# Moving one unit's leftover token rows into a seven-product pass of the last unit, and placing attention visits by phase

## Chip, core and metric

The kernel runs on one core of one Trainium2 chip. The metric is the device time of one execution in microseconds (us). Before the change it is 1392.92 us, the median of three runs from 1391.83 to 1393.26 us.

## What is computed

Attention with normalized queries and keys, followed by a feed-forward network with a squared ReLU. All inputs of the attention are float32; the two weight matrices arrive as 64-bit floats, and the kernel turns them into float32 on the chip.

```python
# q, k, v: 8 batches x 12 heads x 448 rows x 64; g_q, g_k: 64
q_n, k_n = rmsnorm(q, g_q), rmsnorm(k, g_k)
attn = softmax(q_n @ k_n.T / 8)            # per batch and head
x = (attn @ v) as rows of 3584 tokens x 768
h = maximum(x @ w_in, 0)                   # w_in: 768 x 2048
out = (h * h) @ w_out                      # w_out: 2048 x 768
```

## The kernel before, in words

**Units.** Two batches of 448 tokens make a unit, u = 0 to 3. The attention of unit 0 runs alone at the start. After that the feed-forward network of unit u runs on TensorE between the "visits" of the attention of unit u + 1, one or two visits for each pair of heads. The network of unit 3 has no attention left to run beside and comes alone at the end.

**Blocks and phases.** The generator `ffn` (line 943) goes through four blocks of the 2048 hidden columns. A block has a first phase, in which `x @ w_in` makes two by two tiles `hid`, and a second phase, in which `hid @ w_out` is added to accumulators `acc` in SBUF. Both phases use a scheme of seven products in place of eight (Strassen's, in Winograd's form): `PRODUCTS` names them P1 to P7, the banks of PSUM ("roles") that they share, and the sums of the left and right sides that they read. Sums of left sides (S1, S2, S4, and S3 written over a21) are made on GpSimd by `hidden_sum` (line 1141, instructions of line 1151). Those of the weights are made by `make_sum` (line 1508, instructions of line 1514), on VectorE and GpSimd in turn. A float32 matmul shows as two passes in the trace, so a product of the second phase (two matmuls of 384 columns, line 1251) is four passes.

**Rests.** 448 rows are three tiles of 128 and 64 more. The second phase works on pairs of tiles, one of each batch (NT = 3 pairs). The 64 rows left over of each batch are put together as one tile, the unit's rest. Units 1 and 2 store their rests in DRAM block by block (`keep_rests`, line 1173). Unit 3 loads them (`bring_rests`, line 1181), forms their sums on GpSimd (`add_rests`, line 1203) and multiplies the two as one more pair of tiles, tt = NT, after its own three pairs. Units 0 and 3 multiply their own rest without the scheme in `multiply_rest` (line 1165): four parts times two halves, eight matmuls, sixteen passes a block. In unit 0 these open the second phase. In unit 3 they stand in two groups of four matmuls among the products of the first tile pair (`FIRST_OF_BLOCK`).

**The order of the work.** Every engine runs its instructions in the order in which the program emits them. The order is planned with costs: a product of the first phase costs 18, one of the second 10. `run` (line 1586) takes steps of the generator until a sum of costs is reached, and after every step it also lets through one piece of the deep weight forms (lines 1474 and 1492), one sum of weights, delayed work such as loads, and tasks of the attention. `place` (line 1572) says at which cost each visit of the attention stands. For unit 0 the 24 visits stand at equal distances of the whole cost:

```python
if u == 0:
    return COST * x / unit
```

A block of unit 0 costs 502 before the change: 252 for the first phase and 250 for the second, of which 40 are the rest.

**Conversions.** The weights of blocks 1 to 3 are converted to float32 beside unit 0. `convert` (line 1520) splits a piece on ScalarE (lines 1405, 1406, 1408), joins the piece before it on VectorE (lines 1419, 1438), and asks for the load of the piece after next (`load_weights`, lines 1386 and 1391), which is issued two steps later, or at the latest when it is needed. A block has 16 conversions; the list `late` (line 1553) sets the cost at which each is made, 31.4 apart, eight in a second phase and eight in the first phase after it.

Of the kernel before, what the change touches and what calls it, by code (L numbers as in the profile page):

```python
# [14 lines left out]
F32 = mybir.dt.float32  # L15
# [8 lines left out]
P = 128  # L24
# [201 lines left out]
def program(ctx, tc, rows, v, g, wide, ones, moe_w_in, moe_w_out, out, shift):  # L226
# [690 lines left out]
    FIRST_OF_BLOCK = ["P1", "rest0", "P5", "P4", "P6", "P2", "rest1", "P3", "P7"]  # L917
# [8 lines left out]
    COST_SECOND = (NT * 7 + 4) * COST_OUT  # L926
    COST = NF // 2 * 7 * COST_IN + NBLK * COST_SECOND
    COST_SHORT = NT * 7 * COST_OUT
    LATER = NBLK * (7 * 11 * COST_DEEP + COST_SHORT)
    KEPT = range(1, B // 2 - 1)  # L930
    assert len(KEPT) == 2
# [11 lines left out]
    def ffn(u):  # L943

        accs = []
        for blk in range(NBLK):
# [8 lines left out]
            if u == B // 2 - 1:  # L955
                bring_rests(blk)
                add_rests()
# [195 lines left out]
    PARTS = [(0, 0), (1, 0), (0, 1), (1, 1)]  # L1153
    PARTS_BY_ROW = [(0, 0), (0, 1), (1, 0), (1, 1)]

    def out_of(u, blk):
        return [u * NF // 2 + 2 * blk + t for t in range(2)]

    def multiply_rest(u, blk, hid, places, some, acc=None, halves=range(2)):

        w_sb = [out_sb[n] for n in out_of(u, blk)]
        for half in halves:
            ps = places[half][:, 0:HALF]
            for a, t in some:
                nc.tensor.matmul(  # L1165
                    ps, lhsT=hid[a].rearrange("p t e s -> p t (e s)")[:, t, ds(NT * P, P)],
                    rhs=w_sb[t][:, 2 * a + half, :],
                    start=(a, t) == PARTS[0], stop=(a, t) == PARTS[-1],
                )
            if acc is not None:  # L1170
                add_to(acc[:, ts(half, HALF)], ps, blk == 0)
# [9 lines left out]
    def bring_rests(blk):  # L1181

        if not extra:
            for name in ("11", "12", "S3", "22", "S1", "S2", "S4"):
                some = att.tile([P, S], F32, name="wT", tag="wT", bufs=8)
                extra[name] = some[:, 0 : 2 * P].rearrange("p (t n) -> p t n", t=2)
            extra["accs"] = [
                room.rearrange("p x g h d -> p (x g h d)")[:, 0:DM] for room in rows.rooms
            ]
        for u, names in zip(KEPT, (("11", "12"), ("S3", "22"))):  # L1190
            for a, name in enumerate(names):
                nc.sync.dma_start(extra[name], kept[u][blk, :, a])

    def add_rests():
# [10 lines left out]
    def second_products(u, blk, hid, sums_, accs):  # L1205

        split, final = u in KEPT, u == B // 2 - 1
        if blk == 0:
            accs.extend(new_acc() for _ in range(2 * NT if split else 2 * NT + 1))
# [688 lines left out]
```

## Time and profile before

| what | value |
|---|---|
| median of three runs | 1392.92 us |
| the profiled execution: its own time | 1394.38 us |
| the profiled execution: span from first to last instruction | 1392.6 us |
| mean granted TensorE clock in the span | 0.998 |
| TensorE idle, 10 to 150 us (attention of unit 0 alone) | 1.9 us |
| TensorE idle, 150 to 490 us (network of unit 0) | 3.8 us |
| TensorE idle, 490 to 1105 us (units 1 and 2) | 8.3 us |
| TensorE idle, 1105 us to the end (unit 3 and the last stores) | 7.9 us |
| rests of unit 0, line 1165, four blocks | begin at 177.6, 264.7, 356.0, 443.4 us |

How to read it: the span is that of one profiled execution, and 1.8 us lie outside it in that execution's own time. A stage's idle time is its length less the time in which TensorE is busy. In the rows of the trace, "x16" is the number of instructions that were merged; the figure ahead of the engine is the time from the first one's start to the last one's end; a time in brackets is idle time just before, with what ended it. A bank is a bank of PSUM.

### The profile page before, as it was taken

The numbers are of one execution on the slowest core, as the hardware profiler recorded it, in microseconds if no ns is written. First come the engines' busy times: TensorE is split into PE (matmuls) and PEld (weight loads), VectorE is DVE, ScalarE is ACT, GpSimd is POOL, SyncE is SP. The second block draws the span as 40 slices with busy tenths as digits, with TensorE's granted clock in tenths as the row PEclk, the third lists the DMA queues.
The fourth block names the chain that finished last, engine by engine and source line by source line (L and its number), as shares of the span: only waits on it lengthen the run. The fifth ranks groups of instructions, "written<-read, shape, count | busy, mean of one in ns | idle before, by whom it ended". The sixth has DMA issues, their size and how long they took to land.

```text
span 1392.6 us, 19474 instructions
## 1 busy us (share of the span) xinstructions
PE 1363.3 (98%) x6320; PEld 845.7 (61%) x6320; DVE 807.2 (58%) x1635; ACT 608.3 (44%) x1118; POOL 789.6 (57%) x794
## 2 busy tenths in 40 slices
PE   7999999999999999999999999999999999999997
PEld 3333444444444466676758586676768677868684
DVE  4786545867758755555556755455546642445444
ACT  6885477757666244353434244442434032202020
POOL 5668664746656868576667877566745630303030
PEclk9999999999999999999999999999999999999999
DMA  5566746968769875664739475755527442424223
GB/s 147 149 168 169 203 117 159 264 179 219 233 155 284 231 215 162 187 173 141 204 86 279 140 225 149 211 153 176 146 86 239 142 165 103 135 90 149 78 90 100
DMA packets 385588, 233.36 MB, mean 168 GB/s; under 512 B 272452, under 2 KB 354244, under 8 KB 381380
## 3 DMA queue, kind: packets, MB, share of 16 engines
q1 hardware_dynamic: 385184, 231.95, 57.7%
q8 instruction: 52, 0.85, 0.3%
q14 instruction: 60, 0.49, 0.1%
q10 hardware_dynamic: 292, 0.07, 0.0%
HBM read 174.59 MB, written 57.34 MB: 167 GB/s over the span
## 4 chain that ended last, share of the span: by engine, by line
PE 81%; POOL 4%; DVE 4%; DMA 3%; issue 3%; SPq 2%; ACT 2%; POOLq 0%; ACTq 0%; DVEq 0%
PE bank L1251 30%; PE bank L1042 20%; PE bank L986 8%; PE bank L446 5%; PE bank L536 5%; PE bank L550 4%; PE bank L435 4%; PE bank L1165 2%; POOL sum L473 2%; PE bank L585 1%; DMA qk<-in_k_dram 1%; PE bank L611 1%; SPq L326 1%; SPq L318 1%; PE bank L571 1%
## 5 line engine op out<-in xcount | busy, mean ns | idle before, releaser
L1042 PE MATMUL bank<-xT,in_sb 128*128 128x224 f32 x1344 | 289.3, 354 | 2.9 <-ACT part L1031 2.3
L1251 PE MATMUL bank<-out_sb,hid 128*128 128x384 f32 x768 | 272.5, 488 | 2.2 <-POOL out_sb L1514 1.4
L1345 DVE TENSOR_TENSOR acc<-acc,bank 128x384 f32<-128x384 f32 x312 | 166.6, 548 | 164.6 <-PE bank L1251 138.1
L1042 PEld LDWEIGHTS bank<-xT,in_sb 128*128 128x128 f32 x1344 | 252.6, 190 | 15.0 <-ACT wT L454 5.6
L454 ACT ACTIVATE wT<-bank,rr 128x448 f32<-128x448 f32 x288 | 163.5, 631 | 155.1 <-PE bank L435 92.7
L1251 PE MATMUL bank<-out_sb,sums 128*128 128x384 f32 x576 | 207.2, 490 | 1.3 <-DVE acc L1345 0.9
L1251 PEld LDWEIGHTS bank<-out_sb,hid 128*128 128x128 f32 x768 | 144.7, 190 | 104.5 <-issue 5.6
L204 POOL TENSOR_TENSOR rr<-ms,minus_half 128x8 f32<-128x8 f32 (+1 forms) x96 | 146.0, 1521 | 73.7 <-DVE ms L197 63.8
L1251 PEld LDWEIGHTS bank<-out_sb,sums 128*128 128x128 f32 x576 | 107.7, 190 | 86.3 <-issue 4.3
L1027 DVE TENSOR_TENSOR hid<-hid,bank 128x224 f32<-128x224 f32 x312 | 111.0, 383 | 83.9 <-PE bank L1042 79.1
L986 PE MATMUL bank<-xT,in_sb 128*128 128x448 f32 x336 | 131.9, 546 | 0.1
L473 POOL TENSOR_TENSOR sum<-sum,wT 128x448 f32<-128x448 f32 (+1 forms) x96 | 110.6, 1173 | 8.1 <-ACT wT L454 6.6
L986 PEld LDWEIGHTS bank<-xT,in_sb 128*128 128x128 f32 x336 | 62.1, 190 | 69.0 <-issue 60.2
L446 PE MATMUL bank<-qT,kT 64*128 64x448 f32 (+1 forms) x492 | 100.5, 571 | 1.9 <-DVE qT L409 1.1
L473 POOL TENSOR_TENSOR sum<-wT 128x448 f32<-128x448 f32 x48 | 55.8, 1183 | 69.8 <-ACT wT L454 69.8
L1099 ACT ACTIVATE hid<-hid 128x448 f32<-128x448 f32 x96 | 55.0, 573 | 66.7 <-DVE hid L1027 48.5
L435 PE MATMUL bank<-qT,kT 64*64 64x448 f32 x552 | 77.0, 547 | 1.9 <-ACT wT L454 1.9
L1042 PE MATMUL bank<-more,in_sb 128*128 128x224 f32 x288 | 76.2, 357 | 1.4 <-DVE hid L1037 1.4
L550 PE MATMUL bank<-wT,vt 64*64 64x448 f32 x576 | 74.3, 548 | 0.0
L1039 ACT COPY hid<-bank 128x448 f32<-128x448 f32 x24 | 12.8, 532 | 137.3 <-PE bank L1042 137.3
L369 ACT ACTIVATE qT<-qT,g 128x448 f32<-128x448 f32 x34 | 22.6, 665 | 113.7 <-DVE qT L367 113.7
L446 PEld LDWEIGHTS bank<-qT,kT 64*128 64x128 f32 (+1 forms) x492 | 34.9, 166 | 60.4 <-issue 36.8
(140 smaller groups left out, 2059.1 us busy)
## 6 DMA issues: line engine op xcount, KB each, us to landing
out_sb<-out_forms SPq DMA_DIRECT2D x24, 1536.0 KB, 9.9
in_sb<-in_deep SPq DMA_DIRECT2D x64, 384.0 KB, 4.2
in_sb<-in_deep SPq DMA_DIRECT2D x80, 256.0 KB, 4.1
words<-in_moe_w_in_dram SPq DMA_DIRECT2D x32, 384.0 KB, 3.8
words<-in_moe_w_out_dram SPq DMA_DIRECT2D x32, 384.0 KB, 3.6
out_forms<-out_sb SPq DMA_DIRECT2D x8, 1536.0 KB, 7.5
qk<-in_q_dram SPq DMA_DIRECT2D x96, 96.0 KB, 2.6
qk<-in_k_dram SPq DMA_DIRECT2D x96, 96.0 KB, 2.7
```

What stands on the lines that cost most here:

```text
L204: self.nc.gpsimd.tensor_tensor(out=self.rr[i][:, x, 0 : self.count(i)], in0=ms, in1=self.minus_half.to_broadcast(list(ms.shape)), op=ALU.pow,)
L435: nc.tensor.matmul(sc[ds(half * D, D)], lhsT=turned[i, 1][ds(e * D, D), ds(m * P + half * D, D)], rhs=turned[i, 0][ds(e * D, D), :], start ...
L446: nc.tensor.matmul(sc[some], lhsT=turned[p, 1][r, keys], rhs=turned[p, 0][r, :], start=True, stop=True,)
L454: nc.scalar.activation(new_weights((i, m), e), sc, AF.Exp, scale=rows.rr[i][:, 1, 2 * m + e : 2 * m + e + 1],)
L473: nc.gpsimd.tensor_tensor(out=sums[i, e][some], in0=left[some], in1=weights[key_of(i, m), e][some], op=ALU.add)
L536: nc.tensor.matmul(values_bank(i)[ds(e * D, D), :], lhsT=lasts[i % 2][mine, e, :] if m == NJ else values[i][:, m, e, :], rhs=weights[key_o ...
L550: nc.tensor.matmul(bank[ds(e * D, D), :], lhsT=values[i][keys, n, e, :], rhs=weights[(i, n), e][keys], start=n == 0, stop=n == NJ - 1 and ...
L986: nc.tensor.matmul(ps, lhsT=w_sb[:, IN.index(left), c, :], rhs=forms[u, c][right], start=first and c == 0, stop=c == NK - 1, skip_group_ch ...
L1027: nc.vector.tensor_tensor(out=quarter(name, n), in0=quarter(base, n), in1=ps, op=ALU.add)
L1042: nc.tensor.matmul(ps, lhsT=left, rhs=right, start=start, stop=stop, skip_group_check=True)
L1251: nc.tensor.matmul(ps, lhsT=extra[left][:, t] if tt == NT else lefts[left][:, t, ts(tt, P)], rhs=w_sb[t][:, OUT.index(right), :], start=fi ...
L1345: nc.vector.tensor_tensor(out=acc, in0=acc, in1=ps, op=ALU.add)
```

## The change

- Unit 0 no longer multiplies its rest. It stores it in DRAM as units 1 and 2 do, two transfers a block (`KEPT` now takes in unit 0). The delayed entry for it is made at the beginning of the second phase.
- Unit 3 multiplies two pairs of rests, those of units 1 and 2 (tt = NT) and those of units 0 and 3 (tt = NT + 1), both by the seven products. `multiply_rest` is gone. Its tile pairs come in the order NT, 0, 1, NT + 1, 2. The pair NT is multiplied in `FIRST_ORDER`, and after its P1 come the left sums of the block and then the sums of the second pair, four more instructions on GpSimd.
- Unit 3 brings six tiles a block in place of four. The room for the second pair's five tiles comes from buffers `wT`, `qT` and `kT` of the attention.
- The accumulators of the rests of units 0 and 3 move from `acc` to a second part of the rooms of `rows`. Their rows are stored as two transfers of 64 rows for each accumulator, at the end of unit 3 in place of the ends of units 0 and 3.
- In unit 3 all copies out of PSUM in block 0 are ScalarE's; before, those of the first tile pair were VectorE's.
- In unit 0 visits are placed by phase, three at equal distances in each first phase (84 apart) and three in each second phase (70 apart, which is after every seventh product). Conversions are 27.1 apart in second phases and 22.5 apart in first phases, where the eighth now falls 162 into the phase of 252.

```diff
-    COST_SECOND = (NT * 7 + 4) * COST_OUT
-    COST = NF // 2 * 7 * COST_IN + NBLK * COST_SECOND
-    COST_SHORT = NT * 7 * COST_OUT
+    COST_FIRST, COST_SHORT = 2 * 7 * COST_IN, NT * 7 * COST_OUT
+    COST = NBLK * (COST_FIRST + COST_SHORT)
...
-    KEPT = range(1, B // 2 - 1)
+    KEPT, REST_PAIRS = range(B // 2 - 1), ((1, 2), (0, 3))
...
-                bring_rests(blk)
-                add_rests()
+                bring_rests(blk, hid)
+                add_rests(0)
...
             make_sums(0, 1, 2, 3)
-            for some in (PARTS[:3], PARTS[3:]):
-                multiply_rest(u, blk, hid, roles, some, accs[-1] if (1, 1) in some else None)
-                yield len(some) * COST_OUT
-            turn_roles(2, 1, 0)
+            later.append([5, lambda: keep_rests(u, blk, hid)])
...
-                    ps, lhsT=extra[left][:, t] if tt == NT else lefts[left][:, t, ts(tt, P)],
+                    ps, lhsT=lefts[left][:, t, ts(tt, P)] if tt < NT else extra[tt - NT][left][:, t],
...
-        for tt in range(0 if split else NT + final):
-            order = SECOND_ORDER if tt or not u else FIRST_OF_BLOCK
-            for name in order:
...
+        for tt in () if split else (NT, 0, 1, NT + 1, 2) if final else range(NT):
+            for name in FIRST_ORDER if final and tt == NT else SECOND_ORDER:
+                product(tt, name, roles[PRODUCTS[name][0]][:, 0:HALF], nc.scalar)
+                if final and (tt, name) == (NT, "P1"):
+                    yield from sums_behind_first()
+                    add_rests(1)
                     continue
...
-    every = block / ahead
+    every = ((COST_SHORT - 2 * COST_OUT) / (ahead // 2 - 1), (COST_FIRST - 4 * COST_IN) / (ahead // 2))
     late = deque(
-        block + 2 + every * (n - 2 * tile_pieces) for n in range(len(all_pieces) - ahead)
+        n // ahead * block + (COST_FIRST, block)[m] + 2 + every[m] * (n % (ahead // 2))
+        for n in range(len(all_pieces) - ahead) for m in [n % ahead * 2 // ahead]
     )
...
         if u == 0:
-            return COST * x / unit
-        block = LATER // NBLK
...
+            offsets = [COST_FIRST * n // 3 for n in (1, 2, 3)]
+            offsets += [COST_FIRST + COST_SHORT * n // 3 for n in (1, 2, 3)]
+            block = COST // NBLK
```

## The prediction

> **What bounds the kernel now.** I read the page's busy times first.
>
> ```profile
> PE 1363.3 (98%) x6320; PEld 845.7 (61%) x6320; DVE 807.2 (58%) x1635; ACT 608.3 (44%) x1118; POOL 789.6 (57%) x794
> ```
>
> TensorE (PE) is busy 98% of the span, no other engine above 58%. [...] So I looked in the timeline at what follows what.
>
> ```profile
> 1164.11 9.20 PE L1251 MATMUL bank<-out_sb,wT 128*128 128x384 f32 x28
> 1173.13 0.54 PE L1042 MATMUL bank<-xT,in_sb 128*128 128x224 f32 x2
> ```
>
> The pair of rests in unit 3: 28 passes between 1164.11 and 1173.13 us, no idle time in brackets. One pass of 384 columns takes 9.02 / 28 = 0.322 us of TensorE's queue, although a row gives 0.49 us as its mean (neighbours overlap). Weight loads (0.19 us each) lie under it. The row decides: a pass removed from such a stretch is worth 0.322 us, not nothing and not 0.49.
>
> Then the busy times by stretch: first phase of unit 0's block 3, its second phase, block 0 of unit 3.
>
> ```profile
> 399.50:443.40 43.90, 43.90 (x142) 18.90 (x140) 30.63 (x52) 34.24 (x62) 23.48 (x19) 1.00 0.78 217
> 443.40:486.30 42.90, 41.62 (x142) 20.80 (x140) 31.28 (x60) 9.39 (x17) 36.10 (x36) 1.00 0.85 253
> 1102.50:1172.90 70.40, 70.40 (x283) 53.20 (x282) 28.95 (x61) 19.20 (x39) 22.41 (x24) 1.00 0.36 125
> ```
>
> After the stretch and its length the columns are PE, PEld, DVE, ACT and POOL. TensorE fills all three but for 1.28 us in the second. The nearest rivals are ACT in first phases (34.2 of 43.9; 36.1 of 44.1 in block 1, 37.2 of 47.5 in block 2) and POOL in block 3's second phase (36.1 of 42.9).
>
> **The change part by part.**
>
> *Passes.* Unit 0 loses 16 a block, 64 in all. They stand on the path:
>
> ```profile
> 443.42 5.43 PE L1165 MATMUL bank<-out_sb,hid 128*128 128x384 f32 x16
> 448.69 2.74 PE L1251 MATMUL bank<-out_sb,hid 128*128 128x384 f32 x8
> 451.27 2.74 PE L1251 MATMUL bank<-out_sb,sums 128*128 128x384 f32 x8
> 454.36 0.91 PE L1251 MATMUL bank<-out_sb,hid 128*128 128x384 f32 x2 [0.34 <-DVE acc L1345]
> 455.95 0.91 PE L1251 MATMUL bank<-out_sb,hid 128*128 128x384 f32 x2 [0.69 <-POOL out_sb L1514]
> ```
>
> 64 x 0.322 = 20.6 us off. Unit 3 loses its own 16 a block and gains seven products of four passes, 28: 12 x 4 = 48 more, 48 x 0.322 = 15.5 us. Net 16 passes, **-5.2 us**. No other matmul changes, and the instruction orders of units 1 and 2 on TensorE are the same in both programs.
>
> *What the rest covered.* In the rows above, 5.2 us of passes lie between the first phase and the first product that needs a sum. Without them P5 starts 2.58 us after the first phase and its visit end (P1 and P2, 1.29 us each), P6 at 3.87, P4 at 5.16.
>
> Left sums: in block 3, where P1 would start at 443.42, POOL makes S1 from 443.99 to 445.40 and S2 to 446.48; P5 is due at 446.00 and P6 at 447.29. Slack 0.6 and 0.8 us. Block 1 has the same 0.6; blocks 0 and 2 have more. [...] After the change two VectorE derivations of deep forms come back to back at just this place. By the row S1 takes 1.00 us undisturbed and 1.41 in blocks 1 and 3, beside such work, and the slack above has 1.41 in it already. [...] I take 0 by the row, and up to 0.5 us in each of blocks 1 to 3 for the range.
>
> Weight sums: both waits of 0.69 to 0.70 us on POOL's out_sb (blocks 1 and 3) are T4, made after the rest had begun. In the new order the last conversion stands 162 into the first phase and T4 is emitted at its last product, ahead of the left sums on POOL. **-1.4 us**, certain within a few tenths.
>
> Evacuation: with three banks P6 waits for P1's addition to leave its bank, 2.58 us later. VectorE's order at the boundary loses a weight sum and a join (0.55 each) and gains a derivation (0.55); it was done with the visit's work 2.7 us after the boundary (446.1). P1's addition lands at about +2.5 against +3.87. Nothing is added there.
>
> *VectorE's queue in block 3.* SP sends nine piece loads at this boundary, then the blocks for the keys' transpose, which stands in VectorE's queue ahead of additions that free banks:
>
> ```profile
> 446.89 4.59 SPq L892 DMA_DIRECT2D in_sb<-in_deep  x9
> 451.66 1.96 SPq L326 DMA_DIRECT2D qk<-in_k_dram  x2
> ```
> ```profile
> 458.42 0.65 DVE L367 STREAM_TRANSPOSE kT<-qk 128x448 f32<-128x448 f32 x1 [4.12 <-DMA qk<-in_k_dram]
> ```
>
> The blocks land 15.0 us after the boundary. VectorE's 4.12 us of waiting now lie under a visit. In the new order the transpose comes after P4's addition, at +7.1, with P3's and P7's additions behind it; the next tile pair's P2 needs P3's bank at +13.7 (seven products 9.0, visit 3.4, P1 1.3). If the blocks still land at +15.0, P2 waits for the transpose and the addition until 16.3: 2.6 us, and some tenths at P5. But the large store of weight forms that went out just ahead (440.32) now goes out three products earlier, and SP should be through its loads 2 to 3 us sooner: +12.5, no wait. Bounds 0 and 3.5; I take 1.5, less the 0.34 shown above: **+1.2 us**. In blocks 1 and 2 no piece loads lie there, and the blocks are asked for 4 us after the boundary: nothing.
>
> *Conversions closer together.* In first phases of blocks 1 to 3 the steps with a conversion go from 1, 2, 4, 6, 8, 9, 11, 13 to 1, 2, 3, 4, 6, 7, 8, 9. Each load is issued two steps after the conversion two earlier, so four of eight are now issued in the step that needs them. Landing takes 3.6 to 3.8 us (page, part 6), so ACT may wait for them. Cover: the copy behind has 4.7 us (two products) before its bank is needed, later copies 6 to 8 because a visit lies between. Walking ACT's new order with the old durations, it catches up at the visit 15 us in and lags about 3 us by the last conversion, at 30 of 44 us; then it has 14 us without conversions. I take **+0.5 us**, bounds 0 and the rival below. In second phases conversions go from 31.4 to 27.1 apart; ACT has 28.3 us of work at most there, in 37.8: nothing.
>
> *POOL in block 3*: 36.1 us of work in 42.9 - 5.2 = 37.7. It stays under TensorE, but what it makes for unit 1's start comes up to 3 us later against TensorE; there a 1.9 us stall on ACT's weights exists already. I take +0.3, bounds -1 and 2.
>
> *Transfers.* Eight stores of rests (128 KB, 2.0 us) and eight more loads (2.1 us) pass through SP's queue, 16 x 0.6 us. In unit 0 the store is ahead of the q loads of the next pair by 1.2 us; a pair has two visits, 27 us. In unit 3 a block's loads have the whole first phase: nothing. The loads for the next block wait for the pair NT + 1, which ends 9 us before the block does, earlier than now.
>
> *Unit 3 otherwise.* The pair NT comes first, its sums made long before, so P5 no longer needs this block's S1. VectorE gains six additions a block (3.3 us in 74 us with 33 busy), POOL four sums (0.73 each): under TensorE. In block 0 P5's copy on ACT stands behind the last activations: 0 to 0.5 us, I take 0.2.
>
> *The end.* The last accumulator is one transfer of 128 rows, not two of 64 with 0.53 us between issues: **-0.4 us** (bounds -1 and 0).
>
> Sum: -5.2 - 1.4 + 1.2 + 0.5 + 0.3 + 0.2 - 0.4 = **-4.8 us**. On the profiled execution's own 1394.38 us (span 1392.6 and 1.8 around it) that is 1389.6. The median is 1.46 us under that execution, so 1392.92 - 4.8 = **1388.1 us**, -0.34%.
>
> **The rivals.** (The bound of 0.2%, 2.8 us, is about what a measurement of this kernel can tell from no change: 1390.1 to 1395.7.)
>
> A, the forecast: TensorE bounds all stages, small stalls. 1385 to 1390. Chance 0.70.
>
> B, the gain of the second phases is lost: block 3 doesn't shrink because POOL (36.1 us, with 6.8 us of gaps now) or the late transpose holds TensorE to 42.9 us. The transpose's bound of 3.5 and POOL's of 2 are reached: -4.8 + (3.5 - 1.5) + (2 - 0.3) + 0.4 for S1 = -0.7, 1392.2. For it speaks POOL's share, against it that TensorE waited for POOL only 1.4 us in all, in the waits that go. Chance 0.19.
>
> C, slower: the four loads issued in their own step hold ACT up for their whole landing, 4 x 3.7 = 14.8 us in a first phase. ACT then needs 36.1 + 14.8 = 50.9 us of 44.1, and TensorE waits 6.8 us in each of three phases: -4.8 + 20.4 - 0.5 = +15, 1408. It decides the sign when the waits exceed ACT's free 7 us by 1.6 us a phase, over 2.2 us a load. For it speaks that ACT already waits up to 1.6 us there with loads one step ahead; against it that a step lasts 2.4 to 3.3 us and SP runs ahead of the step that emits a load. Chance 0.11, most of it near +4.
>
> The range of eight in ten takes A with the stalls of today going too (-4.8 - 3, 1385.0) and B: 1385.0 to 1392.8. Faster by over 0.2% 0.70, within 0.2% 0.19, slower 0.11.
>
> **What would show it.** Right: TensorE's busy time about 5 us less; second phases of unit 0 near 37.8 us; blocks of unit 3 near 74.3; no waits on POOL's out_sb. Wrong in size: a stall on additions behind the keys' transpose 13 us into block 3's second phase of over 3 us. Wrong in sign: first phases of blocks 1 to 3 over 46 us with ACT waiting for words.

## The result, and the profile after

After the change the kernel takes 1397.95 us (median of seven runs, 1395.28 to 1398.68), before 1393.26 us (median of seven in the same comparison, 1391.83 to 1394.23). The ratio is 1.0029, 95% interval 1.0020 to 1.0038: 0.29% slower, where the prediction said 0.34% faster.

The profiled execution took 1396.01 us, with a span of 1393.8 us. TensorE's busy time (the first figure of the page's row) fell by 2.4 us from 1363.3, about half of the 5.2 us that the prediction wanted:

```profile
PE 1360.9 (98%) x6304; PEld 842.6 (60%) x6304; DVE 817.8 (59%) x1647; ACT 607.6 (44%) x1122; POOL 802.8 (58%) x810
```

The 16 passes are gone (6320 to 6304), so something else grew. The busy times by stretch answer for the same three as before: first phase of unit 0's block 3, its second phase, block 0 of unit 3.

```profile
388.34:433.38 45.04, 44.80 (x142) 19.08 (x140) 31.95 (x53) 33.49 (x61) 26.34 (x22) 1.00 0.86 240
433.38:481.23 47.85, 43.70 (x183) 20.21 (x181) 34.03 (x61) 13.57 (x25) 40.66 (x39) 1.00 0.79 223
1089.28:1164.08 74.80, 74.73 (x295) 55.49 (x294) 28.81 (x61) 21.88 (x45) 28.04 (x32) 1.00 0.36 127
```

(The second stretch holds the visit at the block's end too, 8.5 us; before, it ended ahead of that visit.) Unit 3's block is as predicted. The first phase is 1.2 us longer than before with the same matmuls.

The opening of that second phase, in TensorE's timeline, stands against the five rows shown before:

```profile
433.38 2.85 PE L1238 MATMUL bank<-out_sb,hid 128*128 128x384 f32 x8
436.07 2.74 PE L1238 MATMUL bank<-out_sb,sums 128*128 128x384 f32 x8
438.65 1.45 PE L1238 MATMUL bank<-out_sb,hid 128*128 128x384 f32 x4
...
441.90 1.56 PE L1238 MATMUL bank<-out_sb,hid 128*128 128x384 f32 x4 [0.51 <-DVE acc L1320]
```

The rests are gone, P5 follows 2.7 us behind the start, and the wait on GpSimd's T4 is gone with them. A wait on VectorE's additions is there still (0.51 us; 0.34 before).

Each stage, from its first matmul to the next stage's (us; the unit 0 phases contain their visits, the last one the visit at the end of unit 0):

| stage | before | after | difference | predicted |
|---|---|---|---|---|
| start of unit 0's network | 129.05 | 129.22 | +0.2 | 0 |
| first phases, blocks 0 to 3 | 48.51, 43.85, 45.48, 43.85 | 48.35, 45.87, 47.15, 45.04 | +4.7 | +0.5 |
| second phases, blocks 0 to 3 | 43.27, 45.87, 43.55, 52.87 | 38.11, 41.22, 38.43, 47.84 | -20.0 | -20.5 |
| units 1 and 2 | 606.25 | 608.05 | +1.8 | 0 |
| unit 3 | 282.53 | 298.35 | +15.8 | +15.7 |
| last matmul to the span's end | 7.53 | 6.17 | -1.4 | -0.4 |
| span | 1392.6 | 1393.8 | +1.2 | -4.8 |

So 4.2 of the missing 6 us are in first phases and 1.8 in units 1 and 2. One more thing is in the table. Just before unit 1, TensorE stands still for about 2 us in both kernels, and in the profiled execution of before its clock was then halved for 3.4 us:

```profile
488.70:492.10 3.40, 1.51 (x16) 0.51 (x14) 1.47 (x3) 1.90 (x4) 3.32 (x4) 1.00 0.38 97
492.20:495.60 3.40, 3.40 (x22) 1.25 (x16) 0.00 (x0) 1.50 (x4) 3.32 (x5) 0.50 0.37 61
```

The number behind the five engines is the granted clock: 1.00 in the first row, in which TensorE works 1.51 of 3.40 us, 0.50 in the second. The visit took 9.96 us, against 8.51 after the change, where the clock stayed at 1.00. Without it the second phases gained about 18.3, not 20.0, 2.2 less than predicted. The first profile of after is also a quick one: 1.9 us under its median, where that of before is 1.1 us over the median of this comparison. Its +1.2 us is therefore too small; a second profile (after_again, below) is 4.2 us over before's.

### The profile page after: what moved, and what is told of

The parts are those of the page before. It is cut to its first block, busy times and chain, and to the rows that moved or that the text cites. A ratio compares the mean times of both kernels' runs of the same rounds, so it can differ in the third digit from the quotient of the medians.

```text
span 1393.8 us, 19558 instructions
## 1 busy us (share of the span) xinstructions
PE 1360.9 (98%) x6304; PEld 842.6 (60%) x6304; DVE 817.8 (59%) x1647; ACT 607.6 (44%) x1122; POOL 802.8 (58%) x810
## 4 chain that ended last, share of the span: by engine, by line
PE 77%; DVE 6%; DMA 4%; ACT 3%; POOL 3%; issue 3%; SPq 2%; DVEq 0%; ACTq 0%; POOLq 0%
PE bank L1238 33%; PE bank L1040 20%; PE bank L984 5%; PE bank L446 4%; PE bank L550 4%; PE bank L435 4%; PE bank L536 4%; DMA words<-in_moe_w_out_dram 2%; POOL sum L473 1%; PE bank L585 1%; DVE more L1449 1%; DVE acc L1320 1%; DMA in_sb<-in_deep 1%; DMA qk<-in_k_dram 1%; PE bank L611 1%
## 5 line engine op out<-in xcount | busy, mean ns | idle before, releaser
L1238 PE MATMUL bank<-out_sb,hid 128*128 128x384 f32 x800 | 285.6, 489 | 1.5 <-DVE acc L1320 1.5
L1320 DVE TENSOR_TENSOR acc<-acc,bank 128x384 f32<-128x384 f32 x300 | 159.9, 547 | 146.9 <-PE bank L1238 135.8
L454 ACT ACTIVATE wT<-bank,rr 128x448 f32<-128x448 f32 x288 | 163.8, 630 | 130.5 <-PE bank L435 91.7
L1238 PEld LDWEIGHTS bank<-out_sb,hid 128*128 128x128 f32 x800 | 149.9, 190 | 113.6 <-issue 9.0
L984 PE MATMUL bank<-xT,in_sb 128*128 128x448 f32 x336 | 132.0, 546 | 0.0
L1093 POOL TENSOR_TENSOR hid<-hid 128x448 f32<-128x448 f32 x24 | 27.2, 1140 | 176.5 <-DVE hid L1025 172.1
L446 PE MATMUL bank<-qT,kT 64*128 64x448 f32 (+1 forms) x492 | 104.0, 571 | 3.4 <-ACT qT L369 2.2
L984 PEld LDWEIGHTS bank<-xT,in_sb 128*128 128x128 f32 x336 | 62.0, 190 | 69.1 <-issue 60.1
L446 PEld LDWEIGHTS bank<-qT,kT 64*128 64x128 f32 (+1 forms) x492 | 35.4, 166 | 64.8 <-issue 36.5
```

What stands on the lines that cost most here:

```text
L446: nc.tensor.matmul(sc[some], lhsT=turned[p, 1][r, keys], rhs=turned[p, 0][r, :], start=True, stop=True,)
L454: nc.scalar.activation(new_weights((i, m), e), sc, AF.Exp, scale=rows.rr[i][:, 1, 2 * m + e : 2 * m + e + 1],)
L984: nc.tensor.matmul(ps, lhsT=w_sb[:, IN.index(left), c, :], rhs=forms[u, c][right], start=first and c == 0, stop=c == NK - 1, skip_group_ch ...
L1238: nc.tensor.matmul(ps, lhsT=lefts[left][:, t, ts(tt, P)] if tt < NT else extra[tt - NT][left][:, t], rhs=w_sb[t][:, OUT.index(right), :], ...
L1320: nc.vector.tensor_tensor(out=acc, in0=acc, in1=ps, op=ALU.add)
```

## The experiments

Theories at the beginning. 1: conversions 22.5 apart make ScalarE wait for words, the visit's work stands behind it, and TensorE waits. 2: the rest covered VectorE's work at the boundary. 3: the places of the visits. 4: the new transfers and the new tile in DRAM disturb others. Theory 1 comes in two forms. In 1a the words come late because their load is issued in the very step that needs them; in 1b because the load stands in SP's queue behind other transfers. "Phases" are those of unit 0; times of phases and waits are those of each run's profiled execution, waits for words those of blocks 1 to 3 (215 to 460 us). "The clock was halved for x us" means that the granted clock stood at 0.50 for that time.

| kernel | median us | ratio to before, 95% interval | first phases, blocks 0 to 3 | second phases |
|---|---|---|---|---|
| after | 1397.95 | 1.0029 (1.0020 to 1.0038) | 48.35, 45.87, 47.15, 45.04 | 38.11, 41.22, 38.43, 47.84 |
| conv_even | 1406.27 | 1.0097 (1.0082 to 1.0112) | 48.44, 44.19, 44.94, 44.18 | 38.10, 47.65, 41.94, 53.44 |
| visits_even | 1410.48 | 1.0122 (1.0108 to 1.0137) | 47.16, 48.15, 51.34, 45.74 | 39.21, 41.63, 42.42, 52.67 |
| products_alone | 1416.64 | 1.0167 (1.0151 to 1.0183) | 47.16, 44.30, 48.69, 44.28 | 39.22, 47.69, 46.87, 56.14 |
| placed_alone | 1395.54 | 1.0016 (1.0008 to 1.0024) | 48.46, 45.17, 47.59, 45.17 | 43.27, 44.18, 43.27, 52.68 |
| loads_early | 1397.14 | 1.0024 (1.0015 to 1.0032) | 48.56, 44.96, 45.93, 44.69 | 38.11, 42.63, 38.11, 50.10 |
| conv_mid | 1399.26 | 1.0035 (1.0021 to 1.0049) | 48.37, 45.12, 47.63, 45.15 | 38.11, 43.59, 39.71, 48.03 |
| even_two_sums | 1395.34 | 1.0019 (1.0012 to 1.0026) | 48.44, 44.40, 45.72, 44.41 | 38.11, 42.61, 39.63, 49.39 |
| near_two_sums | 1415.15 | 1.0154 (1.0140 to 1.0169) | 48.43, 54.21, 50.40, 54.71 | 38.11, 40.16, 38.46, 47.35 |
| near_two_sums_early | 1400.08 | 1.0051 (1.0037 to 1.0065) | 48.31, 45.29, 50.41, 44.68 | 38.11, 42.38, 38.47, 49.78 |
| mid_two_sums | 1413.63 | 1.0146 (1.0130 to 1.0162) | 48.38, 55.17, 49.06, 54.67 | 38.11, 39.17, 38.40, 47.04 |
| deep2 | 1407.02 | 1.0094 (1.0079 to 1.0108) | 56.44, 47.28, 51.85, 45.16 | 38.10, 39.76, 38.13, 46.94 |
| raw_spread | 1395.46 | 1.0015 (1.0007 to 1.0023) | 49.59, 45.41, 46.10, 45.24 | 38.10, 40.16, 38.13, 48.50 |
| near_spread | 1397.58 | 1.0027 (1.0019 to 1.0035) | 49.58, 45.25, 48.79, 46.22 | 38.11, 40.52, 38.46, 45.23 |
| near_spread_behind | 1395.40 | 1.0013 (1.0004 to 1.0021) | 48.93, 45.23, 45.57, 45.23 | 38.11, 40.18, 38.45, 47.41 |
| before_spread | 1394.96 | 1.0015 (1.0008 to 1.0022) | 49.53, 44.41, 44.94, 44.41 | 43.27, 46.03, 43.27, 52.10 |
| near_act_stores | 1393.32 | 0.9994 (0.9985 to 1.0002) | 48.14, 45.40, 45.71, 45.25 | 38.11, 40.16, 38.49, 45.76 |
| near_pool_stores | 1411.51 | 1.0122 (1.0106 to 1.0137) | 51.07, 49.47, 49.40, 50.71 | 38.10, 40.18, 39.82, 47.40 |

### The change in its parts

**conv_even**: the conversions of first phases as far apart as before.

```diff
-    every = (..., (COST_FIRST - 4 * COST_IN) / (ahead // 2))
+    every = (..., COST_FIRST / (ahead // 2))
```

> The changed kernel with one term undone: in first phases the eight conversions are spaced 31.5 apart again (before 31.4, after 22.5), so the last stands 222 into the phase of 252. Theory 1 (the denser conversions make ScalarE wait for words, and with it the visit's exponentials and TensorE): the first phases of unit 0's blocks 1 to 3 go back from 45.87, 47.15 and 45.04 us to about 43.9, 45.5 and 43.9, in all 4.7 us less; the waits on T4 in second phases come back (1.4 us), so about 1394.5 us, 3.3 less than after. Theory 2 (the loss sits at the boundary, where the rest no longer covers VectorE's work) or theory 3 (the visits' places): first phases stay within 0.5 us of after's, time 1397.5 to 1399.5. Theory 4 (the new stores and the new tile in DRAM disturb other transfers): 1397 to 1399.

First phases did what theory 1 says (44.19, 44.94, 44.18; all but 0.1 of the 4.9 us in blocks 1 to 3 gone; ScalarE's waits for words of w_out from 26.2 to 9.5 us), and the kernel became 8 us slower all the same. TensorE's waits in unit 0:

```profile
PE bank L1238 <- DVE out_sb L1489: 8.4, 3, 2.9
PE bank L1238 <- POOL out_sb L1489: 5.6, 3, 2.9
```

After the engine and what it waits for come the us in all, the times and the longest. 14.0 us for sums of weights, in blocks 1 to 3, where the theory had booked the old 1.4 for T4. In unit 0 the clock was also halved for 13.7 us, in before's profile for 3.4. So theory 2 had the place right, the boundary; what the rest had covered there were the sums of weights, on VectorE and GpSimd, that the last conversion sets off.

**visits_even**: `return COST * x / unit` for unit 0's visits, conversions as after.

> The changed kernel with another term undone: visits of unit 0 at equal distances of the whole cost (77 apart), conversions as after. Theory 1: conversions still stand 22.5 apart, ScalarE still waits, first phases of blocks 1 to 3 keep at least 3 of their 4.7 us: 1396 to 1398 us. Theory 2: no change at the boundaries with a visit, 1397 to 1399. Theory 3 (three visits a phase at fixed places put a visit beside each batch of waits and at each boundary): first phases back to 43.9, 1393 to 1394.

No theory foresaw this: slower than after by 0.9%. First phases grew to 48.15 and 51.34, with 7.1 us of waiting on exponentials (L454) ahead of L602, the matmul that adds up the exponentials. Visits and conversions are placed for each other, and one alone fits worse.

**products_alone**: both put back, so only the products and the rests are new.

> Rests as after the change (none multiplied in unit 0, a second pair by seven products in unit 3), visits at equal distances of the whole cost and first phases' conversions 31.5 apart, nearly as before. Theory 1: the 5.2 us of sixteen passes are really gained, T4 is waited for as before or more, since the cover is gone: 1387.5 to 1390 us. Theory 2: second phases of unit 0 lose at least 1 us each of their 5.2: 1392 to 1394. Theory 4: units 1 and 2 and the rest lose what they lose after: 1391 to 1393.

All theories missed, by 22 us or more. The gain of 5.2 us in passes turns into a loss. Block 1's second phase on TensorE:

```profile
260.48 3.08 PE L1238 MATMUL bank<-out_sb,hid 128*128 128x384 f32 x8
263.39 0.81 PE L1238 MATMUL bank<-out_sb,sums 128*128 128x384 f32 x2
267.85 2.32 PE L1238 MATMUL bank<-out_sb,sums 128*128 128x384 f32 x4 [3.65 <-DVE out_sb L1489]
271.60 1.62 PE L1238 MATMUL bank<-out_sb,sums 128*128 128x384 f32 x2 [1.43 <-DVE out_sb L1489]
```

P5 comes 2.9 us into the phase and waits 3.65 us for T1, P6 then 1.43 for T2. Before, 5.26 us of rests stood ahead of them. In all TensorE waits 17.2 us for sums of weights (13.8 on VectorE, 3.4 on GpSimd), and in unit 0 the clock was halved for 27.3 us. The two are not added here: time at the halved clock in which TensorE waits would count twice.

**placed_alone**: the kernel before, with the new places of visits and conversions and its old products.

> The kernel before with visits and conversions of unit 0 placed anew alone (three visits in each phase, conversions 22.5 apart in first phases and 32.9 in second phases; rests as before). Theory 1: first phases of blocks 1 to 3 grow by about 4.7 us as after the change, T4 waits go (1.4 us), so about 1396.5 us, slower than before by 0.2%. Theory 2: the rest still covers the boundary, T4 waits go: 1391 to 1392. Theory 4: 1392 to 1393.

Theory 1 held: first phases of blocks 1 to 3 grew by 1.3, 2.1 and 1.3, 4.75 us in all, as after the change; words took 25.3 us of waiting. Block 1's second phase lost its T4 wait (45.87 to 44.18). Slower than before by 0.16%. So the new places cost 4.7 us in first phases by themselves, and the new products cost 23 us without them.

### Between the two

**loads_early**: a join ends ahead of the loads of its step, and `to_load` counts one step, not two.

> The changed kernel with each load of words issued one step earlier (a join ends ahead of the loads of its step, and a load follows one step after the conversion that asks for it, not two). conv_even has shown that ScalarE's waits for words in first phases follow the spacing (26.2 us at 22.5, 9.5 at 31.5). Theory 1a (the words come late because the load is issued in the step that needs them): those waits fall from 26.2 us to 12 or less, first phases of blocks 1 to 3 from 45.9, 47.2, 45.0 to about 44.5, 46, 44.3, time 1394.5 to 1396. Theory 1b (a load lands late because of what stands ahead of it in SP's queue or beside it in the DMA engines): waits stay over 20 us and the time at 1397 to 1399.

First phases as 1a says (44.96, 45.93, 44.69), the waits not (20.1 us), and second phases and unit 1's first block gave it back (42.63, 50.10; the first phase of unit 1's first block 44.24 against 40.21, with a halved clock of 6.8 us in that stretch). That profiled execution took 1402.37 us, 5 us over the median, so it shows the losses larger than usual. Same time as after, within the intervals: the time doesn't decide.

**conv_mid**: `(COST_FIRST - 2 * COST_IN) / (ahead // 2)`, 27.0 apart.

> The changed kernel with first phases' conversions 27.0 apart, between after (22.5) and conv_even (31.5); the last stands 191 into the phase. Theory 1 with the cover of theory 2 (dense conversions make ScalarE wait for words, late ones make P5, P6 and P4 wait for sums of weights that the rest used to cover): waits for words about 15 us, first phases 2 us shorter in all than after, waits for sums of weights 0 to 2 us (T4 is made two products into the second phase, ahead of P4's turn): 1395 to 1397. If the second phase's loss begins as soon as any sum is made behind the boundary: 1400 or more.

A miss, 2.3 us over the range: waits for words stayed at 21.2 us although every load is now issued a step ahead. That speaks against 1a as the whole cause. Waits for sums were 1.7 us, within what was expected.

**even_two_sums**: conv_even with two sums in each step.

```diff
-            make_sum()
+            for _ in range(2):
+                make_sum()
```

> conv_even (31.5 apart) with two sums of weights in each step in place of one, so T1, T3 and T2, T4 come in two steps, not four. In conv_even TensorE waited 14.0 us for sums of weights. If they were late because the program emits one a step: waits under 4 us, second phases near 38.5, 41, 39, 49.5, time 1393 to 1396. If VectorE and GpSimd themselves have no room at the boundary: waits of 8 us or more, 1400 to 1405.

11 us faster than conv_even. Waits for sums fell from 14.0 to 6.2 us, between the two answers: most of it was the order in which the program emits them.

**after_again**: the changed kernel, a second profile.

> The changed kernel again, for a second profile: its median is 1.9 us over the profiled execution. If the difference is due to stalls that vary, they show in first phases of unit 0 or in waits for pieces in units 1 and 2 (0.9 and 0.6 us longer than before in the first profile); the phases of unit 3 and all of TensorE's own times should be the same to 0.1 us.

1398.9 us, with a span of 1396.8 us. Unit 3 is the same to 0.1 us. The clock was halved for 3.4 us at 481.4, at the end of unit 0, just as in before's profile, so this is the fairer one to set against before: start +1.1 us, first phases +5.7, second phases -18.3 (49.57 in block 3), units 1 and 2 +1.2, unit 3 +15.8, the end -1.4. That is +4.2 us in all, and the ratio of the medians (1.0029) makes 4.0. The halved clock does not explain by itself why the median lies 1.9 us over the first profile: of the seven executions, those of 1397.94, 1398.61 and 1398.68 us show the same mean clock of 0.999 as the profiled one of 1396.01.

**near_two_sums** (29.25 apart, two sums) and **mid_two_sums** (27.0 apart, two sums) were meant to be the best of both.

> The changed kernel with first phases' conversions 29.25 apart and two sums of weights a step. In even_two_sums (31.5 apart) T1 was emitted behind P1 of the second phase and TensorE waited 6.2 us for sums; at 29.25 T1 and T3 are emitted in the first phase's last step, T2 and T4 behind P1. Theory (the loss is the cover that the rest gave to late sums, on one side, and ScalarE's waits for words, on the other): waits for sums 0 to 2 us, waits for words about 11 us, first phases of blocks 1 to 3 near 44.6, 46, 44.6 us, second phases near 40, 38.5, 48: 1390.5 to 1393, faster than after by 5 us and at most level with before. If VectorE's instructions are held up beside GpSimd's at the boundary whatever the order: 1395 to 1397, as even_two_sums.

> Conversions 27.0 apart and two sums a step: all four sums are emitted in the first phase, so no sum can be late. If late sums are the larger part of what is left: below near_two_sums by 1 us. If ScalarE's waits for words are: first phases as in conv_mid (45.1, 47.6, 45.2), 1394 to 1396, above near_two_sums.

Both missed their times by about 20 us. Second phases were right (40.16, 38.46, 47.35 and 39.17, 38.40, 47.04), and the first phases of blocks 1 and 3 took 54 to 55 us. In near_two_sums, SP's queue and then ScalarE, block 1:

```profile
224.16 2.48 SPq L1439 DMA_DIRECT2D in_deep<-in_sb  x3
226.68 2.83 SPq L1441 DMA_DIRECT2D in_deep<-in_sb  x2
229.61 1.46 SPq L1366 DMA_DIRECT2D words<-in_moe_w_out_dram  x1
```
```profile
236.29 0.54 ACT L1380 ACTIVATE words<-words 128x384 f32<-128x384 f32 x1 [7.96 <-DMA words<-in_moe_w_out_dram]
```

Five raw stores hold SP's queue from 224.2 to 229.5 us, the load of words behind them is issued over 229.6 to 231.1, and ScalarE waits 7.96 us for it. TensorE waits 7.3 us for the query that stands behind it, and the clock is then halved for 6.8 us. The sums being done one step sooner had moved the raw stores right ahead of a load. After the change they stood just behind one (227.6) and ahead of the next (235.2), which cost 4.05 us.

**near_two_sums_early**: the same, loads a step earlier.

> The same with each load of words issued a step earlier, which in loads_early took 2.5 us off the first phases of blocks 1 to 3 and put 3.3 us on second phases and the start of unit 1. At 29.25 every load is already issued at least a step ahead of its conversion. Theory 1a: words' waits fall by 3 us or more, time 1 us under near_two_sums. Theory 1b (SP's queue and the landing set it): same within 0.1%, or later where the load now stands ahead of the q and k loads.

15 us faster than near_two_sums, where 1 was expected: first phases of blocks 1 and 3 are back at 45.29 and 44.68. Load and raw stores had changed places: the load was issued at 225.77 us, the raw stores at 227.16 to 232.9.

**deep2**: two steps of the deep forms in each step, in place of one.

> The changed kernel with two steps of the deep forms in each step of the program in place of one, so that they are over before the boundary. After the change two derivations at block 1's boundary took 2.57 us on VectorE and P1's addition came at +3.3 us; its second phase took 41.2 us where 39.0 would be its instructions' own time. Theory 2 (these derivations at the boundary hold up VectorE): second phases of blocks 1 and 3 shorter by 1 to 2 us each, 1394.5 to 1396.5. Theory 1 (the words' loads, with more stores of deep forms ahead of them in SP's queue): first phases longer, 1398 or more.

Theory 2 holds for its place: second phases of blocks 1 and 3 went from 41.22 to 39.76 and from 47.84 to 46.94. The whole is 9 us slower, and block 0's first phase (56.44 us against 48.35) shows most of it:

```profile
152.94 0.69 DVE L1449 TENSOR_TENSOR more<-in_sb 128x512 f32<-128x512 f32 x1 [8.09 <-DMA in_deep<-more]
```

A derivation waited 8.09 us in VectorE's queue for the store that frees its buffer, and TensorE waited 5.5 us for the `hid` behind it.

### SP's queue

Open was why the words come late, 1a or 1b. **raw_spread**, **near_spread** and **before_spread** (after, near_two_sums and before) send out the five raw stores one a step, each beside a derivation:

```diff
+            if raws:
+                nc.sync.dma_start(*raws.popleft())
             if len(to_keep) > 1 or not make:
                 nc.sync.dma_start(*to_keep.popleft())
```

> The changed kernel; the five raw stores of deep forms (L1439, L1441), which go out in one step and hold SP's queue for 6 us (229.0 to 235.1 in block 1), go out one in each of five steps, each beside a derivation. Theory 1b (the words come late because of what stands ahead of their load in SP's queue): the longest wait for words in block 1's first phase falls from 4.1 us to 2.5 or less, first phases of blocks 1 to 3 lose 2 to 4 of their 4.7 us, and one step fewer is left for the boundary: 1393 to 1396. Theory 1a (issued in the step that needs them, whatever stands ahead): at most 1 us, 1397 to 1399.

> near_two_sums with the five raw stores spread. There the second phases were as short as the prediction wanted them (38.1, 40.2, 38.5, 47.4 us), and the first phases of blocks 1 and 3 took 54.2 and 54.7, with one wait for words of 8.0 us: the raw stores went out one step sooner, right ahead of a load. Theory 1b: first phases near 44.5, 46, 44.5, second phases as in near_two_sums: 1390 to 1393, level with before or faster. Theory 1a, or a cause of the 8 us other than these stores: 1405 or more.

> The kernel before with its five raw stores spread. In block 1 they went out at 232.2 to 237.8 us, 0.9 us behind a load of words and 4 us ahead of the next one, so they stood in no load's way: same as before within 0.1%, 1392 to 1394, by theory 1b. If spreading helps by itself (fewer derivations left for the boundary, shorter bursts on the DMA engines): 1390 to 1392.

1b holds for the loads that stood behind raw stores. raw_spread is about 2 us faster than after (1.0015 against 1.0029), words' waits 15.6 us (26.2). near_spread's first phases of blocks 1 and 3 fell from 54.21 and 54.71 to 45.25 and 46.22, 17.5 us by the order of five stores; about 3.3 of them are the halved clock behind the stalls (30 matmuls of L984 took 12.80 and 13.39 us there, else 11.47). It missed its time all the same. First phases of blocks 1 to 3 came out 5.3 us over what was expected, 2.8 of it in block 2, where the clock was halved for 3.4 us; and the first phases of the first blocks of units 1 and 2 took 41.25 and 39.58 us, 3.0 over before (TensorE waited 3.3 us for pieces of deep forms). before_spread missed too: 0.15% slower than before, where the same time was expected. Its waits for words of w_out fell from 7.9 to 2.8 us, but block 0's first phase grew by 1.0 us and those of blocks 1 and 3 by 0.6 each, so spreading isn't good by itself.

**near_spread_behind**: the step of the deep forms stands behind the loads and conversions of its step.

> near_spread with the step of the deep forms (a raw store, the store of a derivation and the next derivation) behind the loads and the conversion of its step, not ahead of them. Theory 1b: a load of words has nothing of its own step ahead of it in SP's queue, waits for words fall by another 2 to 5 us and the time by 0 to 1.5 us against near_spread; but ScalarE and VectorE get the derivation behind the join, so nothing else should move. If SP's order is not what holds the words: same as near_spread.

2.2 us under near_spread, more than expected, and not by the expected way: words' waits for w_out did not fall (16.2, 13.9 there). Block 2's first phase went from 48.79 to 45.57; about half of this is a halved clock that did not come again, the rest a shorter wait for exponentials ahead of L602.

**near_act_stores** and **near_pool_stores**: near_spread_behind with all stores of deep forms from ScalarE's queue (`nc.scalar.dma_start`) or GpSimd's (`nc.gpsimd.dma_start`).

> near_spread_behind with all fifteen stores of deep forms of a block (five raw, ten derived) issued from ScalarE's queue in place of SP's. With them spread in SP's queue, waits for words in blocks 1 to 3 were 16.2 us and first phases 45.2, 45.6, 45.2 us, 0.8 to 1.4 above before. Theory 1b (SP's queue is all of it): waits for words under 9 us, first phases at most 44.4, 45, 44.4, time 1 to 2.5 us under near_spread_behind: 1393 to 1394.5. Rival: a store waits in ScalarE's queue for its derivation on VectorE, and exponentials and copies behind it wait too: 1396 or more. Theory 1a (the load's own landing of 3.7 us against steps of 2.4 us): no change of waits, 1395 to 1396.

> The same fifteen stores issued from GpSimd's queue, which in first phases is busy 23.5 of 43.9 us. Theory 1b: waits for words under 9 us, first phases at most 44.4, 45, 44.4, time 1393 to 1394.5. Rival: issuing a store takes GpSimd long, or a store waits there for its derivation, and the sums of exponentials and the left sums at the boundary come late: second phases over 41 us, 1397 or more.

From ScalarE: 1393.32 us, level with before (0.9994, 0.9985 to 1.0002) and 0.35% under after (0.9994 / 1.0029). Waits for words of w_out fell from 16.2 to 3.5 us as 1b says. First phases of blocks 1 and 3 stayed at 45.3 and 45.4, which neither theory says; what holds them is in the next section. From GpSimd: issuing a store took 0.8 to 1.6 us there, first phases took 49 to 51 us, and TensorE waited 8.9 us for scaled queries. In block 1 VectorE's transposition of the query ended 4.2 us after the scores had begun, behind an instruction of a join (L1394) that took 3.22 us, against 0.35 at 231.62 us in after; what held it was not tried. No version here beats the kernel before by more than the measurement can tell.

## Why the prediction was wrong, step by step

**Passes, right.** A pass costs 0.322 us at both ends: block 0's second phase lost 5.16 us (16 passes), and unit 3 gained 15.8 where 15.5 and 0.2 were summed.

**T4's waits (-1.4), right, at a price booked elsewhere.** They are gone in after and in placed_alone. They go because the conversions come earlier. The prediction took this from the emission order and did not ask what the other sums would do without it; products_alone shows 17.2 us. "What the rest covered" asked the right question and answered it only for the new places.

**Conversions closer together (+0.5), the step that failed.** Measured +4.9 us in the first phases of blocks 1 to 3 (placed_alone +4.75, with the old products; in conv_even all but 0.1 of it is gone). Taken from the start of one group of matmuls to the start of the next, the 4.9 us lie at two kinds of place: 2.6 in the scores (L446) of the second visit of blocks 1 and 3 (1.4 and 1.2), behind the scaling of the query (L369), and 2.3 ahead of L602 in blocks 1 and 2 (0.6 and 1.7), behind the exponentials. The walk along ScalarE's order looked only at the copies behind a conversion, which have 4.7 us or more. It left out the scaling and the exponentials, which a visit needs at once. ScalarE after the change, block 1:

```profile
226.44 0.51 ACT L993 COPY part<-bank 128x448 f32<-128x448 f32 x1
229.72 0.57 ACT L1380 ACTIVATE words<-words 128x384 f32<-128x384 f32 x1 [2.77 <-DMA words<-in_moe_w_out_dram]
230.18 0.55 ACT L1381 ACTIVATE words<-words 128x384 f32<-128x384 uint32 x1
230.76 1.07 ACT L1383 ACTIVATE words<-words 128x384 f16<-128x384 f32 x1
231.58 0.62 ACT L369 ACTIVATE qT<-qT,g 128x448 f32<-128x448 f32 x1
```

and TensorE there after, then before:

```profile
229.91 1.92 PE L446 MATMUL bank<-qT,kT 64*128 64x448 f32 x8
232.25 0.97 PE L446 MATMUL bank<-qT,kT 64*64 64x448 f32 x4 [0.42 <-ACT qT L369]
```
```profile
235.06 1.94 PE L446 MATMUL bank<-qT,kT 64*128 64x448 f32 x12
```

The wait for words (2.77 us) and the split (1.9 us) stand ahead of the scaling, which comes 1.67 us after the scores began, against 0.20 before. The bracket shows 0.42 us of idle time; from the first of the twelve passes to the next instruction it is 3.25 us against 1.87, so the loss is 1.38. Not all of it is ScalarE's. The scaling reads what VectorE has transposed; that transposition after, then before:

```profile
230.12 0.63 DVE L367 STREAM_TRANSPOSE qT<-qk 128x448 f32<-128x448 f32 x1
```
```profile
234.59 0.64 DVE L367 STREAM_TRANSPOSE qT<-qk 128x448 f32<-128x448 f32 x1
```

It ends 0.84 us after the scores began, against 0.17 before, behind the joins of the denser conversions. ScalarE's split adds the other 0.83 us.

The place ahead of L602 is the same kind further on. SP's queue and ScalarE in block 1, after the change:

```profile
223.59 0.86 SPq L326 DMA_DIRECT2D qk<-in_k_dram  x2
225.98 0.35 SPq L1366 DMA_DIRECT2D words<-in_moe_w_out_dram  x1
...
229.03 3.73 SPq L1439 DMA_DIRECT2D in_deep<-in_sb  x3
232.81 2.25 SPq L1441 DMA_DIRECT2D in_deep<-in_sb  x2
235.18 1.35 SPq L1366 DMA_DIRECT2D words<-in_moe_w_out_dram  x1
```
```profile
242.28 0.55 ACT L1380 ACTIVATE words<-words 128x384 f32<-128x384 f32 x1 [4.05 <-DMA words<-in_moe_w_out_dram]
...
251.01 2.18 ACT L454 ACTIVATE wT<-bank,rr 128x448 f32<-128x448 f32 x4
```

The load at 235.18 us went out directly behind the raw stores. ScalarE waited 4.05 us for it, three splits followed close together, and the exponentials behind them began 4.7 us after their scores, against 1.3 before. So this loss comes by SP's queue (1b). The load at 225.98 us, behind which the scaling waited, had no other transfer ahead of it: SP was through with the keys' load at 224.45 and, by the trace, waited for a join on VectorE, which ended at 225.95. It was issued in the step of its own conversion, the third (1a). The argument against rival C that "SP runs ahead" did not hold there.

The experiments agree. With the stores off SP's queue (near_act_stores) the loss ahead of L602 is gone, and that in the scores stays (1.5 and 1.4 us): the scaling comes 1.79 us after the scores began. There VectorE holds it, whose transposition ends 1.61 us after the scores began, behind joins and derivations, one of them of 1.63 us. With the loads a step earlier (loads_early) the loss in the scores falls to 1.1 and 0.8. No run took the joins off VectorE alone.

Rival C had the right place and sign. It was to decide the sign from 1.6 us a phase, which is what was measured, and had most of its chance near +4. Two of its readings were off: by its own figures ScalarE had 44.1 less 36.1, or 8.0 us free, not 7, which spoke a little more against it; and ScalarE's longest wait for words in a first phase before was 4.01 us (block 2, at 340.45 us), not 1.6, which spoke for it. The waits for words were given a cover, but of the work behind them only the copies were asked, and VectorE's joins not at all.

**Evacuation ("nothing is added there"), wrong by 1.5 us in block 1.** VectorE at that boundary, which is at 261.55 us:

```profile
262.38 2.57 DVE L1449 TENSOR_TENSOR more<-in_sb 128x384 f32<-128x384 f32 x2 [0.94 <-DMA in_deep<-more]
264.87 0.54 DVE L1320 TENSOR_TENSOR acc<-acc,bank 128x384 f32<-128x384 f32 x1
```

The two derivations take 1.28 us each, not 0.55, the first after 0.94 us of waiting for its buffer, and P1's addition ends at +3.86, not +2.5. P6, due at +3.87, still got its bank; the additions behind P1's came late too, and TensorE waited for two of them:

```profile
267.36 1.56 PE L1238 MATMUL bank<-out_sb,hid 128*128 128x384 f32 x4 [0.33 <-DVE acc L1320]
269.46 1.56 PE L1238 MATMUL bank<-out_sb,sums 128*128 128x384 f32 x4 [0.54 <-DVE acc L1320]
```

deep2, which takes the derivations away from here, made this phase 1.46 us shorter. In before, where they stood ahead of GpSimd's left sums (263.32 and 264.82 us), two derivations of this size took 0.55 and 0.52 us; here GpSimd made S1 (1.00 us, from 262.25) and S2 (1.20) in the same time. What made them long was not shown: no run took GpSimd's work away.

**VectorE's queue in block 3 (+1.2), right in kind and size; two losses beside it were missed.** The keys' transposition came 14.5 us after the boundary, close to the forecast's late case of 15.0, and the four products around the addition behind it lost 1.1 us start to start (0.67 in brackets). In the phase there are two more losses, which the prediction did not have: 0.8 us in the opening products (0.51 in brackets), and 1.8 us at a query that VectorE transposed at 461.2 us, 1.4 us after the scores of its visit had begun; those scores took 3.66 us, not 1.87. near_spread, with the same products and a clock of 1.00 there, took 45.23 us in place of 47.84.

**Left sums (0), GpSimd in block 3 (+0.3)**: TensorE waited for neither in after (up to 0.5 us for S1 and S2 in each of blocks 1 to 3 was the author's estimate; S1 took 1.00 us in blocks 1 and 3, not 1.41, and S2 1.20, not 1.00); the stall ahead of unit 1 went from 1.89 to 2.12 us. **The end (-0.4)**: -1.4, beyond its bounds of -1 and 0; this was not followed up.

**Units 1 and 2, not in the sum: +1.8.** Orders on TensorE are the same; the loss is in the first phase of the first block of each (40.21 and 39.37 us against 39.29 and 38.57), in waits for pieces of deep forms. It varies: in after_again the same two took 38.47 and 40.48, the second with a wait on GpSimd. Kernels with the old rests had 38.6 to 39.3 in unit 1's and 38.6 to 39.0 in unit 2's, those with the new ones 38.5 to 44.2 and 38.6 to 43.1 (the 44.2 with a halved clock). conv_even and products_alone, which have the new store and tile, had 38.6 to 39.0, so theory 4 isn't borne out there. The cause is open.

Sum: +4.2 in conversions, +0.5 in second phases (2.2 without before's halved clock), +1.8 in units 1 and 2, +0.2 at the start, -0.9 in unit 3 and the end: 5.8 of the 6.0 us that the first profile missed. From the second profile, which has before's halved clock too: +5.2, +2.2, +1.2, +1.1 and -0.9, 8.8 of 9.0 us.

## What to carry to other kernels

Work that is taken off the path may be the cover of something late: list who is due in the first microseconds behind it, with the old placing and the new one, because 5.2 us of rests stood over sums of weights for which TensorE would have waited 17. When an engine gets more work ahead of a point in its order, as ScalarE did here, whose split put a scaling off by 0.83 us, go through every consumer behind it, the one with the shortest slack first, and do so for each engine that gets more work; here a 0.6 us scaling and the exponentials mattered and the copies didn't. Bursts of stores in a queue that also loads are worth placing by hand: five stores ahead of one load or behind it made 17 us of difference over two phases, the halved clock behind the stalls included.

## What the runs showed of the hardware

- A stall of TensorE of about 2 us can cost 1.7 us more (an estimate: half of 3.41 us; block 3's second phase was 1.73 us longer in after_again): the granted clock then stood at 0.50 for 3.41 us (before at 492.2, after_again at 481.4), and for 6.83 or 10.24 us behind the 7.3 us stalls of near_two_sums (236.3, 417.3; mean granted clock of that execution 0.991, of after's 0.999). It doesn't come each time: the same stall of 2.1 us left the clock at 1.00 in the first profile of after. What decides whether it comes was not shown.
- Where matmuls overlap, the idle time in brackets understates a stall: 0.42 us shown, 1.38 us lost.
- Issuing a raw store held SP's queue for 0.8 to 1.4 us (near_two_sums: 2.48 us for three, 2.83 for two). A load of words took 0.35 us at 225.98 in after, and 1.35 directly behind the stores.
